# Gated linear attention and a mixture of experts on one core: scores ahead of the key transposes, ranks two steps late, first scans and checks by tile, and later weights

## The chip, the core and the metric

The kernel runs on one core of one Trainium2 chip. A core has five engines, each with an instruction queue of its own: TensorE (PE in the profile, with its weight loads as PEld), VectorE (DVE), ScalarE (ACT), GpSimd (POOL) and SyncE (SP), which here only issues transfers. Transfers are carried out by 16 DMA engines. The metric is the device time of one execution, in microseconds (us).

## What is computed

```python
def _attn_ref(q, k, v, alpha):            # each (4, 8, 768, 48): batch, head, time, width
    for t in range(S):
        state = alpha[:, :, t, :, None] * state + np.einsum('bhd,bhe->bhde', k[:, :, t], v[:, :, t])
        y[:, :, t] = np.einsum('bhd,bhde->bhe', q[:, :, t], state)

def _moe_ref(x, w_skip, w_gate, w1, w2):  # x: 3072 rows of 384
    do_compute = x @ w_skip > 0
    xc = x[do_compute]
    e_idx = np.argmax(xc @ w_gate, axis=1)                 # one of 8 experts
    gate_w = softmax(xc @ w_gate)[e_idx]
    for e in range(E):
        h = np.maximum(xc[mask] @ w1[e], 0.0)              # 384 -> 1024
        y[mask] = gate_w[mask, None] * (h @ w2[e])         # 1024 -> 384
    out[do_compute] = xc + y                               # the other rows stay x
```

The rows of attention, heads side by side, are the x of the experts.

## The kernel before

**Tiles.** Time is cut into 6 chunks of 128. A tile i is one chunk (i // 4) of one batch (i % 4) with all its 8 heads: 24 tiles. Two tiles make a pair j = i // 2, 12 pairs, and four tiles make a cycle, after which the next chunk of the same batch follows. Eight heads lie as four columns (p) of two partition halves (h): 48 rows from partition 0, 48 from partition 64, so that 112 partitions are spanned.

**A tile's arithmetic.** Scans over the decays give their running products from the left (`prefix`, tile pfx) and from the right (`suffix`, sfx), both on the DVE. GpSimd multiplies k by sfx (`scale_k`) and q by pfx (`scale_q`). Then PE computes k times q (`scores`, into ps_s), the DVE copies its causal part through a mask into the buffer st (`causal`), PE adds st times v (`intra`) and q times the state of the earlier chunks (`inter`) into ps_y. For the state, PE turns k (`turn_k`: transposes into ps_k, which ACT copies to kt), multiplies kt by v (`outer`, into ps_v), and the DVE adds the old state and multiplies by the chunk's total decay (`carry`). Of the output, ACT copies ps_y to xt, PE turns it to rows (`rows`, again into ps_k, of which there is one buffer), ACT copies it to x, and SP stores x.

**Routing.** Tiles are routed in groups (four at a time up to tile 16, then smaller). `logits` multiplies xt by the gate's weights wg, `route` takes nine short DVE instructions and one exponential on ACT (called one at a time by `tick`), `rank` counts with PE which place of its expert's list each row has, `slots` turns that into addresses, and `scatter` (GpSimd, an indirect DMA) writes row numbers into the lists xs in DRAM. `inspect` adds up on ACT how far the decays of a pair lie outside 0 to 1, two operations over 112x1024 into a scratch tile junk; the sums decide at the end whether a general path has to run (it doesn't here).

**Experts.** After the last tile `experts` loads the lists (`metas`), gathers the listed rows from the output (`gather`), turns them (`turn`), and computes `up` and `down` for each expert, 1 first. Weights come by `fetch` (raw pieces of 384 KB) and are split by `split` into a high part (ACT) and a low part (DVE or GpSimd). Each of the products with the experts' weights is three products of parts.

**Order.** The program is scheduled by hand: every engine carries out its instructions in the order in which the code issues them. `attention_begin` sets up and starts pair 0 and pair 1, then `step(i)` is called for the 24 tiles. In step i stand, in this order: on even i the loads of pair j + 3, the store of tile i - 2, one weight piece, turn_k, scores and causal of tile i + 1, on even i suffix and scale_k of pair j + 2, then inter(i), logits where a group is complete, outer(i), intra(i), rows(i - 1), on odd i prefix, scale_q, carry and inspect (of pair j + 3), the route, and at last rank and slots of a group that was complete one step before, and scatters. `constants_late` comes before inspect of the first three pairs, at the end of `attention_begin`. w1 and w2 of the first expert are fetched from step 3 on, w1 split on GpSimd from step 8 on, and the second w1 is fetched from step 22 on, behind the stores of those steps in SP's queue. The names in the order below end in numbers that mark a buffer (dec_138, _139 and _140 are the three decay buffers).

Of the kernel before, what the change touches and what calls it, by code (L numbers as in the profile page):

```python
# [10 lines left out]
F32 = mybir.dt.float32  # L11
# [12 lines left out]
P = 128  # L24
# [38 lines left out]
class Kernel:  # L63
# [12 lines left out]
    def constants_first(self):  # L76
# [9 lines left out]
        self.odd = const.tile([P, 2, NJ], F32, name="odd")  # L86
# [22 lines left out]
    def constants_late(self):  # L109
# [22 lines left out]
        self.wg = const.tile([P, NP, 32], F32, name="wg")  # L132
        nc.gpsimd.memset(self.wg, 0.0)
        for h in range(2):
            nc.sync.dma_start(out=self.wg[64 * h:64 * h + D, :, 0:E + 1], in_=self.w9[h])

# [14 lines left out]
    def constants_slots(self):  # L151
# [5 lines left out]
        nc.gpsimd.tensor_copy(self.slots1, slots_i)  # L157

# [55 lines left out]
    def scan_pools(self, st):  # L214
# [6 lines left out]
        self.junk = sfix.tile([P, NS, P], BF16, name="junk")  # L221
# [37 lines left out]
    def load_qk(self, j, t=None):  # L259
        nc, w = self.nc, self.pair(j)  # L260
        flat = w["qk"].rearrange("p t a s -> p t (a s)")
        for t in range(2) if t is None else (t,):
            if j < NFIRST:
                nc.sync.dma_start(out=flat[:PD, t], in_=self.qk0[j, :, t])
            else:
                for h in range(2):
                    nc.sync.dma_start(out=flat[64 * h:64 * h + D, t], in_=self.qk[j - NFIRST, h, :, t])
# [17 lines left out]
    def prefix(self, j, t0=0, t1=2):  # L285
# [7 lines left out]
        nc.vector.memset(dec[:, :, 0:1], 0.0)  # L293
# [15 lines left out]
    def inspect(self, j):  # L309

        dec = self.pair(j)["dec"][:PD, 0:2 * W1].rearrange("p (a s) -> p a s", s=SEG)[:, :, 2:]
        for n, (scale, bias) in enumerate(((1.0, -1.0), (-1.0, 0.0))):
            self.nc.scalar.activation(out=self.junk[:PD], in_=dec, func=AF.Relu, scale=scale, bias=bias,  # L313
                                      accum_out=self.odd[:PD, n, j:j + 1])
# [67 lines left out]
    def carry(self, j):  # L382
# [6 lines left out]
        if 2 * j >= B:  # L389
            nc.vector.tensor_tensor(pv, pv, state, ALU.add)  # L390
        nc.vector.tensor_tensor(state, pv, self.pair(j + 2)["total"][:PD].to_broadcast([PD, NS, D]), ALU.mult)
# [237 lines left out]
    def metas(self):  # L629

        self.meta = self.mp.tile([P, E, NB, 2], F32, name="meta")
        for e in (1, 0, *range(2, E)):
# [283 lines left out]
    def attention_begin(self):  # L916
        nc = self.nc
        for t in range(2):
            self.load_dec(0, t)
            self.load_qk(0, t)  # L920
        self.load_dec(1)
        self.load_v(0)
        self.load_qk(1)
        self.load_v(1)
        self.warm_up(WARM0)
        self.constants_scan()
        self.constants_pool()
        self.clear_buffers()
        self.load_dec(2)
        self.load_qk(2)  # L930
        self.load_v(2)
        for t in range(2):
            self.suffix(0, t, t + 1)
            self.scale_k(t)
            self.prefix(0, t, t + 1)
            self.scale_q(t, nc.vector)
            if t == 0:
# [220 lines left out]
```

## Time and profile before

| | |
|---|---|
| median of 3 runs | 332.57 us (331.17 to 335.27) |
| the profiled run | 332.18 us, its span 330.4 us |
| PE busy | 279.1 us (84%) |
| DVE busy | 211.4 us (64%) |
| ACT busy | 150.5 us (46%) |
| POOL busy | 127.0 us (38%) |
| transfers | 56.52 MB, mean 171 GB/s |

The span is what the profiler saw of one execution, from the first to the last instruction; the run's time holds a little more around it. Busy shares are averages over stages with different limits, so they say little by themselves. The views that follow later are: busy time by window, an engine's waits with what ended them, the chain of work that ended last, groups of equal instructions, the timeline of an engine, and the table of DMA issues. In them L323 is line 323 of the kernel before, `a<-b` is what an instruction writes and reads, and the clock is the share of TensorE's full speed that was granted.

### The profile page before, as it was taken

The page shows a single profiled execution, that of the slowest core. Times are in us where ns is not written, and L with a number is a line of the kernel's source. Part 1 is how long each engine was busy: PE and PEld are TensorE (multiplying, and loading weights), DVE is VectorE, ACT ScalarE, POOL GpSimd, SP SyncE. Part 2 cuts the span into 40 slices and gives each one's busy share as a digit, 9 for nine tenths or more (in the row PEclk, how much of TensorE's full clock was granted, in tenths as well). Part 3 has the DMA queues.
Part 4 walks back from the last instruction along what each step waited for, and adds up shares of the span by engine and source line. Part 5 has one row for each costly group of instructions (what it writes and reads, how often), then busy time and mean ns, then how long its engine had stood idle before and what let it go on. Part 6 is the DMA issues. An engine that isn't in the chain of part 4 may idle for free.

```text
span 330.4 us, 7415 instructions
## 1 busy us (share of the span) xinstructions
PE 279.1 (84%) x2937; PEld 254.8 (77%) x2937; DVE 211.4 (64%) x362; ACT 150.5 (46%) x333; POOL 127.0 (38%) x134
## 2 busy tenths in 40 slices
PE   8705895997797789598999579999999999999990
PEld 8604674776576667487799479999999999999990
DVE  5951796477677657668553665757585787758530
ACT  6155655255354254434430733736464637465510
POOL 3390355265656548557271165050403122110111
PEclk9955999599799699779999699999999999999996
DMA  7989989599887574011264097383939284755000
GB/s 192 264 203 243 216 227 290 154 226 257 211 199 202 170 151 125 27 41 35 67 152 101 2 284 273 113 301 115 307 103 320 112 279 180 222 205 192 35 26 19
DMA packets 28379, 56.52 MB, mean 171 GB/s; under 512 B 7192, under 2 KB 13792, under 8 KB 28336
## 3 DMA queue, kind: packets, MB, share of 16 engines
q1 hardware_dynamic: 25392, 50.89, 54.6%
q0 software_dynamic: 2944, 5.07, 4.4%
q8 instruction: 25, 0.41, 0.6%
q14 instruction: 18, 0.15, 0.2%
HBM read 49.09 MB, written 8.50 MB: 174 GB/s over the span
## 4 chain that ended last, share of the span: by engine, by line
PE 62%; DMA 11%; issue 8%; ACT 6%; DVE 5%; POOL 5%; SPq 0%; POOLq 0%; DVEq 0%
PE ps_o L691 19%; PE ps_h L676 18%; PE ps_s L323 6%; PE ps_y L362 5%; DMA xs<-idg,slot 4%; DMA dec<-in_dec_dram 3%; ACT junk L313 3%; PE ps_y L353 3%; PE ps_k L336 3%; PE ps_v L379 2%; DVE pfx L296 2%; DMA qk<-in_qk_dram 2%; PE ps_n L428 2%; POOL xs L518 1%; DMA xr<-out_dram,meta 1%
## 5 line engine op out<-in xcount | busy, mean ns | idle before, releaser
L329 DVE COPY_PREDICATED st<-mask,ps_s 128x1024 f32<-128x1024 uint8 x24 | 31.5, 1315 | 37.3 <-PE ps_s L323 37.2
L700 POOL DMA_INDIRECT out_dram<-o,meta x16 | 16.1, 1004 | 97.0 <-DVE o L698 96.4
L691 PE MATMUL ps_o<-w2h,hh 128*128 128x384 f32 x128 | 44.6, 349 | 3.2 <-ACT w2h L609 3.2
L691 PE MATMUL ps_o<-w2l,hh 128*128 128x384 f32 x128 | 44.3, 346 | 0.4 <-DVE w2l L611 0.3
L691 PE MATMUL ps_o<-w2h,hl 128*128 128x384 f32 x128 | 43.9, 343 | 0.0
L680 ACT ACTIVATE hh<-ps_h 128x512 fp32r<-128x512 f32 x32 | 19.2, 599 | 47.2 <-PE ps_h L676 47.2
L307 POOL TENSOR_TENSOR qk<-qk,sfx 112x512 f32<-112x512 f32 x24 | 28.0, 1183 | 32.4 <-issue 13.2
L303 POOL TENSOR_TENSOR qk<-qk,pfx 112x512 f32<-112x512 f32 x22 | 25.5, 1179 | 36.9 <-DVE pfx L296 36.9
L681 DVE SCALAR_TENSOR_TENSOR hl<-ps_h,hh 128x512 fp32r<-128x512 f32 x32 | 22.1, 692 | 27.4 <-ACT hh L680 27.3
L366 ACT COPY xt<-ps_y 112x256 f32<-112x256 f32 x48 | 15.5, 376 | 51.2 <-PE ps_y L362 51.2
L611 DVE TENSOR_TENSOR w2l<-raw,w2h 128x512 fp32r<-128x512 f32 x48 | 31.5, 683 | 8.3 <-ACT w2h L609 8.3
L676 PE MATMUL ps_h<-xh,w1h 128*128 128x256 f32 x192 | 33.6, 284 | 0.6 <-ACT xh L576 0.6
L676 PE MATMUL ps_h<-xh,w1l 128*128 128x256 f32 x192 | 33.4, 283 | 0.0
L676 PE MATMUL ps_h<-xl,w1h 128*128 128x256 f32 x192 | 33.4, 283 | 0.0
L323 PE MATMUL ps_s<-qk 48*128 48x128 f32 x384 | 31.7, 310 | 1.1 <-POOL qk L303 0.6
L609 ACT CAST w2h<-raw 128x512 fp32r<-128x512 f32 x48 | 28.0, 617 | 8.4 <-DMA out_dram<-x 8.4
L362 PE MATMUL ps_y<-st,v 128*64 128x128 f32 x384 | 31.8, 304 | 0.0
L279 DVE TENSOR_TENSOR_SCAN sfx<-dec,ps_t 112x1041 f32<-112x1041 f32 (+2 forms) x13 | 27.8, 2141 | 4.4 <-DMA dec<-in_dec_dram 2.8
L336 PE MATMUL ps_k<-ident,qk 112*128 112x112 f32 x80 | 12.4, 281 | 21.4 <-issue 16.0
L323 PEld LDWEIGHTS ps_s<-qk 48*128 48x128 f32 x384 | 26.6, 210 | 4.7 <-POOL qk L303 0.8
L541 POOL DMA_INDIRECT xr<-out_dram,meta x18 | 20.1, 1119 | 24.7 <-DVE hl L681 13.8
L296 DVE TENSOR_TENSOR_SCAN pfx<-dec,ps_t 112x1040 f32<-112x1040 f32 (+1 forms) x13 | 28.0, 2154 | 1.1
(156 smaller groups left out, 570.6 us busy)
## 6 DMA issues: line engine op xcount, KB each, us to landing
raw<-in_w_dram SPq DMA_DIRECT2D x64, 384.0 KB, 4.5
qk<-in_qk_dram SPq DMA_DIRECT2D x32, 192.0 KB, 6.5
v<-in_v_dram SPq DMA_DIRECT2D x12, 384.0 KB, 7.0
out_dram<-x SPq DMA_DIRECT2D x24, 192.0 KB, 4.1
qk<-in_qk_dram SPq DMA_DIRECT2D x8, 448.0 KB, 9.9
dec<-in_dec_dram SPq DMA_DIRECT2D x12, 232.8 KB, 4.9
dec<-in_dec_dram SPq DMA_DIRECT2D x12, 229.2 KB, 5.1
out_dram<-xr SPq DMA_DIRECT2D x3, 192.0 KB, 4.8
```

Of the source, the lines that this page charges most:

```text
L279: self.nc.vector.tensor_tensor_scan(w["sfx"][:PD, s][:, ::-1], w["dec"][:PD, s][:, ::-1], self.top[:PD].to_broadcast([PD, s.stop - s.start ...
L296: nc.vector.tensor_tensor_scan(w["pfx"][:PD, s], w["dec"][:PD, s], self.top[:PD].to_broadcast([PD, s.stop - s.start]), 1.0, ALU.mult, ALU.max)
L303: (eng or self.nc.gpsimd).tensor_tensor(w["qh"][:PD], w["qh"][:PD], w["pfx"][:PD], ALU.mult)
L307: (eng or self.nc.gpsimd).tensor_tensor(w["kh"][:PD], w["kh"][:PD], w["sfx"][:PD], ALU.mult)
L323: nc.tensor.matmul(ps[:, h, p * P:(p + 1) * P], lhsT=kh[r, p, :], rhs=qh[r, p, :], start=True, stop=True)
L329: self.nc.vector.copy_predicated(w["st"], self.mask, w["ps"])
L336: nc.tensor.transpose(ps[:, p, :], w["kh"][:PD, p, :], self.ident[:PD, :PD])
L362: nc.tensor.matmul(self.place(i, h, p), lhsT=w["v"][:, o:o + 64], rhs=w["st"][:, h, p * P:(p + 1) * P], start=(i < B and p < 2), stop=(p > ...
L609: nc.scalar.copy(out=hi[:, s], in_=raw[:, s])
L611: eng.tensor_tensor(lo[:, s], raw[:, s], hi[:, s].bitcast(F32), ALU.subtract)
L676: nc.tensor.matmul(ps[:, u, :], lhsT=a[:, k, f * P:(f + 1) * P], rhs=b[:, k, :], start=(n == 0), stop=(n == len(order) - 1))
L691: nc.tensor.matmul(ps, lhsT=a[:, f, js], rhs=b[:, f, :], start=(n == 0), stop=(n == 3 * FT - 1))
```

## The change

It moves much and computes the same. In the order of the program:

- q and k are laid out in DRAM so that a row of a transfer is 2 KB (q or k of one tile) where it was 4 KB (both). For pairs 0 and 1 each is a transfer of its own, k first; later pairs keep two transfers per tile, each now with two rows of 2 KB per partition. The gate's weights wg are padded on the host and come as one load, where GpSimd cleared the tile and two loads filled it.
- `constants_late` moves ahead of the scans, and in `attention_begin` pair 0 and pair 1 are scanned by tile; the second half of pair 1 is scanned in step 0 and the suffix of pair 2 in step 1. scale_q of tile 1 goes from the DVE to GpSimd.
- `prefix` writes its zero column with an ACT copy in place of a DVE memset.
- `inspect` takes one tile (112x512) in each step, where it took a pair in each second one.
- In each step scores come before turn_k.
- For the groups up to tile 16, rank and slots come two steps after the group is complete, between inter and outer, where they came one step after it, at the step's end. The DVE finishes the route (`tick(99)`) at each odd step.
- In `carry` the DVE adds, and GpSimd multiplies by the total.
- The first expert's weights are fetched from step 9 on, one piece a step, and w1 is split from step 19 on with the DVE, four calls a step. The second w1 is fetched in `experts`, behind the loads of the lists of experts 1 and 0 and ahead of those of the other six.

```diff
     def prefix(self, j, t0=0, t1=2):
...
-        nc.vector.memset(dec[:, :, 0:1], 0.0)
+        nc.scalar.copy(out=dec[:, :, 0:1], in_=nc.const_aps.tensor(0.0, [PD, (t1 - t0) * NP, 1], F32))
...
-    def inspect(self, j):
+    def inspect(self, i):
-        dec = self.pair(j)["dec"][:PD, 0:2 * W1].rearrange("p (a s) -> p a s", s=SEG)[:, :, 2:]
+        j, t = divmod(i, 2)
+        dec = self.pair(j)["dec"][:PD, t * W1:(t + 1) * W1].rearrange("p (a s) -> p a s", s=SEG)[:, :, 2:]
...
     def carry(self, j):
...
-        if 2 * j >= B:
-            nc.vector.tensor_tensor(pv, pv, state, ALU.add)
-        nc.vector.tensor_tensor(state, pv, self.pair(j + 2)["total"][:PD].to_broadcast([PD, NS, D]), ALU.mult)
+        total = self.pair(j + 2)["total"][:PD].to_broadcast([PD, NS, D])
+        if 2 * j < B:
+            nc.vector.tensor_tensor(state, pv, total, ALU.mult)
+            return
+        nc.vector.tensor_tensor(state, pv, state, ALU.add)
+        nc.gpsimd.tensor_tensor(state, state, total, ALU.mult)
...
     def step(self, i):
...
-        if i == 3:
+        if i == 9:
             self.fetches = chain(self.fetch(0, "w1"), self.fetch(0, "w2"))
...
-        if i == LATE + 4:
-            self.fetches = self.fetch(1, "w1")
-        for _ in range(2 if i >= LATE + 4 else 1):
-            next(self.fetches, None)
+        next(self.fetches, None)
...
-        if i == 8:
-            self.splits = self.split(0, "w1", nc.gpsimd)
+        if i == LATE + 1:
+            self.splits = self.split(0, "w1", nc.vector)
...
         if i + 1 < NT:
+            self.scores(i + 1)
             self.turn_k(i + 1)
-            self.scores(i + 1)
             self.causal(i + 1)
...
         self.inter(i)
...
+        done = ends.get(i - 2)
+        if done and done[1] < LATE:
+            self.tick(99)
+            self.rank(done)
+            self.small = self.slots(done)
         g = ends.get(i)
         if g:
             self.logits(g)
         self.outer(i)
...
             self.carry(j)
-            if j + 3 < NJ:
-                self.inspect(j + 3)
+        for n in (i + 2, i + 4) if i < 2 else (i + 4,):
+            if n < NT:
+                self.inspect(n)
...
         done = ends.get(i - 1)
-        if done:
+        if done and done[1] >= LATE:
...
-        self.tick(99 if i >= LATE else 3 if t else 1)
-        if i >= 8:
+        self.tick(99 if t or i >= LATE else 1)
+        for _ in range(4):
             next(self.splits, None)
...
     def experts(self):
-        self.metas()
+        self.metas((1, 0))
+        for _ in self.fetch(1, "w1"):
+            pass
+        self.metas(range(2, E))
```

On ACT, at the end of the first tiles' setting up, the order before is this (rtot is the reciprocal total that `prefix` keeps, L118 to L121 are late constants, L313 is inspect, L338 the copy of turned keys):

```order
L295 COPY rtot<-dec_139 112x8
L118 CAST tri<-tri_f 128x128
L119 CAST one_b<-ones_f 128x128
L120 ACTIVATE tri_n<-tri_f 128x128
L121 ACTIVATE one_n<-ones_f 128x128
L313 ACTIVATE junk,odd<-dec_138 112x1024 x2
L313 ACTIVATE junk,odd<-dec_139 112x1024 x2
L313 ACTIVATE junk,odd<-dec_140 112x1024 x2
L338 COPY kt<-ps_k 128x448
L366 COPY xt<-ps_y 112x256 x2
```

And this is it in the changed kernel (L295 writes a zero column, L297 rtot, L316 is inspect, L341 the copy of turned keys):

```order
L121 ACTIVATE one_n<-ones_f 128x128
L295 COPY dec_138<-const-float32-0.0 112x4
L297 COPY rtot<-dec_138 112x4
L341 COPY kt<-ps_k 128x448
L295 COPY dec_138<-const-float32-0.0 112x4
L297 COPY rtot<-dec_138 112x4
L316 ACTIVATE junk,odd<-dec_138 112x512 x2
L295 COPY dec_139<-const-float32-0.0 112x4
L297 COPY rtot<-dec_139 112x4
L316 ACTIVATE junk,odd<-dec_138 112x512 x2
L341 COPY kt<-ps_k 128x448
```

The constants now lie ahead of the first scan's zero column, looks of one tile lie between the scans, and the copy of turned keys no longer has six looks at whole pairs ahead of it.

On PE, where the first group is ranked, the order before has the rank at the end of step 5, ahead of the transposes and scores of tile 7 (tiles 6 and 7 are in qk_104):

```order
L493 MATMUL ps_n<-mg_287,one_b 128x8
L494 LDWEIGHTS tri
L494 MATMUL ps_n<-mg_287,tri 128x32
L336 MATMUL ps_k<-ident,qk_104 128x112 x4
L323 MATMUL ps_s<-qk_104 128x128 x8
L353 MATMUL ps_y<-qk_104,state_110 64x128 x8
```

In the changed kernel (L404 is rows, L326 scores, L339 turn_k, L356 inter, L494 on the rank):

```order
L404 MATMUL ps_k<-ident,xt 128x112 x4
L326 MATMUL ps_s<-qk_104 128x128 x8
L339 MATMUL ps_k<-ident,qk_104 128x112 x4
L356 MATMUL ps_y<-qk_104,state_110 64x128 x8
L494 LDWEIGHTS one_b
L494 MATMUL ps_n<-base_row,one_b 128x32
```

Scores stand between the rows of the tile before and the transposes, and the rank has moved behind scores, transposes and inter of step 6.

On SP, at the end of attention, the order before is this (L411 stores a tile, L535 loads the first expert's list early, L597 fetches a weight piece, L633 loads the lists):

```order
L535 DMA meta_1878<-xs 128x2x2
L411 DMA out_dram<-x 128x384
L597 DMA raw<-in_w_dram 128x768 x2
L411 DMA out_dram<-x 128x384
L597 DMA raw<-in_w_dram 128x768 x2
L411 DMA out_dram<-x 128x384 x2
L633 DMA meta<-xs 128x2x2 x8
L597 DMA raw<-in_w_dram 128x768 x40
```

In the changed kernel (L417 stores, L541 the early list, L603 fetches, L640 lists):

```order
L541 DMA meta_1905<-xs 128x2x2
L417 DMA out_dram<-x 128x384 x4
L640 DMA meta<-xs 128x2x2 x2
L603 DMA raw<-in_w_dram 128x768 x4
L640 DMA meta<-xs 128x2x2 x6
L603 DMA raw<-in_w_dram 128x768 x40
```

The four pieces of the second w1 have moved behind the last four stores and the first two lists.

More of the change, by code (lines that the diff above doesn't have):

```diff
@@ L157, in constants_slots, with load_gates @@
         nc.gpsimd.tensor_copy(self.slots1, slots_i)
+    def load_gates(self):
+        self.wg = self.const.tile([P, NP, 32], F32, name="wg")
+        self.nc.sync.dma_start(out=self.wg[:PD], in_=self.w9)
     def clear(self):
@@ L220, in scan_pools @@
         self.sfxp = pool("sfxp", 3)
-        self.junk = sfix.tile([P, NS, P], BF16, name="junk")
+        self.junk = sfix.tile([P, NP, P], BF16, name="junk")
     def clear_buffers(self):
@@ L627, in expert_pools, with metas @@
             self.nc.vector.memset(t, 0.0)
-    def metas(self):
-        self.meta = self.mp.tile([P, E, NB, 2], F32, name="meta")
-        for e in (1, 0, *range(2, E)):
+    def metas(self, experts):
+        if 1 in experts:
+            self.meta = self.mp.tile([P, E, NB, 2], F32, name="meta")
+        for e in experts:
             ins = self.nc.sync.dma_start(out=self.meta[:, e], in_=self.slot_rows(e))
@@ L931, in attention_begin @@
         self.load_v(2)
[L932 to L937, printed above, removed]
-                self.turn_k(0)
-                self.scores(0)
-                self.warm_up(WARMB)
-        self.causal(0)
-        self.suffix(1)
-        for t in (2, 3):
-            self.scale_k(t)
-        self.prefix(1)
-        for t in (2, 3):
-            self.scale_q(t)
-        self.constants_late()
-        for j in range(3):
-            self.inspect(j)
+        self.suffix(0, 0, 1)
+        self.scale_k(0)
+        self.prefix(0, 0, 1)
+        self.scale_q(0, nc.vector)
+        self.scores(0)
+        self.turn_k(0)
+        self.warm_up(WARMB)
+        self.suffix(0, 1, 2)
+        self.scale_k(1)
+        self.prefix(0, 1, 2)
+        self.scale_q(1)
+        self.causal(0)
+        self.inspect(0)
+        self.suffix(1, 0, 1)
+        self.scale_k(2)
+        self.prefix(1, 0, 1)
+        self.scale_q(2)
+        self.inspect(1)
         self.todo, self.fetches, self.splits = [], iter(()), iter(())
@@ L983, in step @@
         if i + 1 < NT:
+            self.scores(i + 1)
             self.turn_k(i + 1)
-            self.scores(i + 1)
             self.causal(i + 1)
-        if t == 0:
-            if j + 2 < NJ:
-                self.tick(2)
-                self.suffix(j + 2)
-                for n in range(2):
-                    self.scale_k(2 * j + 4 + n)
+        if i == 0:
+            self.suffix(1, 1, 2)
+            self.scale_k(3)
+            self.prefix(1, 1, 2)
+            self.scale_q(3)
+        if i == 1:
+            self.scan_right(2)
+        if t == 0:
+            self.tick(2)
+            if i > 0 and j + 2 < NJ:
+                self.scan_right(j + 2)
             self.tick(2)
@@ L1002, in step @@
         self.outer(i)
+        if done and done[1] < LATE:
+            self.tick(99)
+            self.todo += range(*done)
         if g and g[0] >= LATE:
@@ L1134, in layouts @@
     w9n = w9.reshape(KT, P, E + 1).transpose(1, 0, 2)
-    w9 = w9.reshape(NP, 2, D, E + 1).transpose(1, 2, 0, 3)
+    w9p = np.zeros((PD, NP, 32), w9.dtype)
+    for h in range(2):
+        w9p[64 * h:64 * h + D, :, 0:E + 1] = w9.reshape(NP, 2, D, E + 1)[:, h].transpose(1, 0, 2)
     nat = np.stack([alpha, k, q, v], axis=2).reshape(B, NP, 2, 4, S, D).transpose(0, 1, 3, 2, 5, 4)
```

47 lines of the change are left out of this document (27 added, 20 removed).

## The prediction

> **What bounds the kernel now.** I read the busy time by stage first, then TensorE's waits, then the chain of work and the queues at each wait. The first table cuts the span by stage; its columns are the window, its length, the busy time and count of PE, PEld, DVE, ACT and POOL, the granted clock, the DMA engines' share and GB/s.
>
> ```profile
> 0.00:51.90 51.90, 34.36 (x429) 29.69 (x433) 32.34 (x34) 26.25 (x62) 22.54 (x37) 0.84 0.90 230
> 51.90:130.20 78.30, 63.05 (x986) 51.56 (x989) 53.52 (x76) 36.05 (x89) 44.28 (x42) 0.89 0.77 199
> 130.20:172.60 42.40, 36.99 (x526) 30.89 (x522) 27.53 (x75) 16.61 (x46) 24.05 (x23) 0.92 0.23 58
> 172.60:199.40 26.80, 21.55 (x126) 20.16 (x127) 14.70 (x28) 9.35 (x18) 8.38 (x9) 0.87 0.48 132
> 199.40:330.40 131.00, 123.18 (x882) 122.50 (x880) 83.30 (x151) 62.26 (x118) 27.72 (x26) 0.98 0.52 176
> ```
>
> The edges are the masked copies (L329) of tiles 6 and 18, and the first instructions of up for the first and the second expert. So attention's start takes 51.9 us for six tiles, three cycles of four tiles take 78.3 (26.1 each), the last six tiles 42.4, the join of attention and experts 26.8, the experts' body 131.0. The body is full of PE work and the diff doesn't touch it. In the other stages no engine is full, so waits carry them.
>
> TensorE's waits (total, times, longest):
>
> ```profile
> PE ps_k L336 <- issue: 16.0, 5, 13.6
> PE ps_n L488 <- DVE sl L473: 13.3, 4, 3.3
> PE ps_o L691 <- ACT w2h L609: 3.2, 1, 3.2
> ```
>
> One of 13.6 us in the start; four of 3.3 at the rank of a group; one of 3.2 in the join. What the wait of 13.6 stands on is seen on ACT, where the copy of turned keys that frees `ps_k` stands behind six junk operations of inspect:
>
> ```profile
> 27.93 0.19 ACT L313 ACTIVATION_READ_ACCUMULATOR junk<-dec 112x1 f32 x1
> 28.02 0.51 ACT L338 COPY kt<-ps_k 128x448 f32<-128x448 f32 x1
> ```
>
> Clock and transfers in three windows, same columns as above:
>
> ```profile
> 28.60:34.60 6.00, 5.96 (x54) 5.16 (x55) 2.90 (x4) 1.19 (x4) 0.00 (x0) 0.50 1.02 251
> 58.50:65.30 6.80, 6.80 (x69) 5.56 (x68) 3.56 (x3) 1.18 (x3) 1.07 (x1) 0.50 0.55 163
> 192.90:194.90 2.00, 0.34 (x4) 0.10 (x2) 1.97 (x5) 0.48 (x1) 1.53 (x2) 1.00 1.01 373
> ```
>
> After the long wait, and after a rank's wait of 3.3, PE runs at clock 0.50 for six or seven us. After the gap of 1.9 us that ends at 194.9 it doesn't (1.00). The Trainium skill, "TensorE: Matmul & The Clock Gate", section "Why this matters for your kernels", asks for no idle gap above some 3 us; the trace agrees, with 3.3 on one side and 1.9 on the other.
>
> **The start.** The DVE has 32.34 us of work before tile 6's copy and can begin when the first decay is in:
>
> ```profile
> 3.79 1.24 DVE L279 TENSOR_TENSOR_SCAN sfx<-dec,ps_t 112x521 f32<-112x521 f32 x1 [2.76 <-DMA dec<-in_dec_dram]
> ```
>
> The change takes one multiply off it (`scale_q(1)`, of 512 columns like the split's subtraction in the row below, 0.68) and the memsets (an estimate of 0.4), so 31.2 us are left.
>
> ```profile
> L611 DVE TENSOR_TENSOR w2l<-raw,w2h 128x512 fp32r<-128x512 f32 x48 | 31.5, 683 | 8.3 <-ACT w2h L609 8.3
> ```
>
> Moved ahead of the scans, the late constants put four casts on ACT before the first zero column; inspect by tile halves what one look blocks ACT for. The new wait is that each prefix scan follows an ACT copy of the zero column, in ACT's order. My count over the six first prefixes of what the scan waits there: 2.1 behind clears and casts, 1.2 behind the first `kt`, then 0.4, 0.6 and 1.1 behind row copies and looks, 5.4 in all. 3.8 + 31.2 + 5.4 = 40.4 for tile 6, against 51.9: -11.5. That is if loads keep up. The window moved 230 x 51.9 = 11.9 MB. Three weight pieces of 0.39 MB leave it (w1(0) and w2(0) now begin in step 9), so 10.7 remain, and at the saturated 251 GB/s of 28.6 to 34.6 these take 42.6: -9.3. I take -9.5, since the q and k pieces at issue are the very loads of that window; bounds -4 (a wait of some 5 us for loads stays) and -11.5. The tile's transposes behind its scores, and `wg` as one load (SP no longer waits for GpSimd's memset), lie under the scans.
>
> **The three cycles.** A row of the chain is start, length and what ran:
>
> ```profile
> 74.11 0.54 PE ps_v L379 x13
> 74.64 0.95 PE ps_y L362 x16
> 75.59 0.53 PE ps_k L398 x4
> 76.12 0.11 PE ps_n L438
> 76.24 0.54 issue
> 76.77 0.57 PE ps_k L336 x4
> 77.35 1.09 PE ps_s L323 x16
> 78.44 0.60 PE ps_y L353 x16
> ```
>
> The 0.54 of issue is the copy of x out of the one `ps_k` buffer, ahead of the transposes. With scores first it is covered by scores (1.09): 0.5 less in each step whose chain runs there, two in four. At the rank the chain is:
>
> ```profile
> 56.23 1.15 ACT junk L313 x2
> 57.38 0.09 ACT ex L470
> 57.47 0.02 issue
> 57.49 0.19 DVE mg L472
> ```
>
> The exponential stands behind four instructions of inspect. Two steps late the ranks wait for less, and for the DVE rather than ACT. DVE's pieces in these cycles, and GpSimd's:
>
> ```profile
> L329 DVE COPY_PREDICATED st<-mask,ps_s 128x1024 f32<-128x1024 uint8 x13 | 17.1, 1316 | 23.4 <-PE ps_s L323 23.3
> L296 DVE TENSOR_TENSOR_SCAN pfx<-dec,ps_t 112x1040 f32<-112x1040 f32 x6 | 13.9, 2320 | 0.6
> L279 DVE TENSOR_TENSOR_SCAN sfx<-dec,ps_t 112x1041 f32<-112x1041 f32 x6 | 13.8, 2303 | 0.0
> L391 DVE TENSOR_TENSOR state<-ps_v,sfx 112x384 f32<-112x384 f32 x6 | 3.4, 559 | 0.2
> ```
> ```profile
> L307 POOL TENSOR_TENSOR qk<-qk,sfx 112x512 f32<-112x512 f32 x13 | 15.1, 1183 | 13.9 <-issue 9.9 <-DVE sfx L279 2.8 <-PE ps_n L438 1.2
> ```
>
> A new loop sets the period of a pair. At an odd step the scores end; then turn 0.57, inter 0.60, outer 0.54, intra 0.95, rows 0.53 on PE, the copy of x 0.5 (the 0.54 above) and the zero column 0.2 (as the accumulator's 0.19) on ACT, 3.9 with handover. Only then can the prefix scan start; before, it needed no PE result of the step. Then reciprocal 0.2 and scan 2.32, the carry's add 0.55, the next masked copy 1.32, which frees `ps_s`, and scores 1.09: 9.4 us a pair. One pair of a cycle carries nine short route instructions on the DVE (0.19 each, 1.5 of them in the loop), 10.9; the other carries logits on PE, half of their 1 us hidden, 9.9. A cycle is 20.8, and 3 x (26.1 - 20.8) = -15.9. In it the rank still waits some 2 us: PE is there 5.5 us after the odd scores' end (next scores at 4.3, then turn and inter 1.2), the route's result at 7.4. That is on the harmless side of the clock's edge. GpSimd's new multiply is estimated at 1183 x 384 / 512 = 0.89 a pair, ends long before the inter that reads the state, and with two scalings of k and q each (4 x 1.18) and scatters leaves GpSimd under 8.5 of 10 us. I take -15. Bounds -18 (no wait in the rank) and -8 (each prefix waits 0.8 more, and each rank's wait again halves the clock for 5 us: 6 x 0.8 + 3 x 2.5 = 12, less what overlaps).
>
> **Tiles 18 to 23 and the join.** Tiles 18 to 20 hold one pair of the cycle's kind, which 2.5 us leave by the same loop. w1(0)'s split moves from GpSimd in step 8 on to the DVE in steps 19 to 23: 6 or more of its subtractions are no longer covered by a waiting engine, x 0.68, less what lies in DVE's 35% of idle time: +1.5 (0.5 to 4). Together -1, bounds -2.5 and +2.
>
> In the join, the raws of w1(1) are issued before the last stores:
>
> ```profile
> 169.28 0.92 SPq L597 DMA_DIRECT2D raw<-in_w_dram  x2
> 170.30 0.86 SPq L411 DMA_DIRECT2D out_dram<-x  x2
> ```
> The chain then runs from the last scatter over the meta to the gather:
>
> ```profile
> 173.93 11.71 DMA xs<-idg,slot
> ...
> 186.10 1.78 DMA meta<-xs
> ...
> 190.07 4.74 DMA xr<-out_dram,meta
> ```
> The table of DMA issues has the median of all scatters (count, us to landing):
>
> ```profile
> xs<-idg,slot POOLq DMA_INDIRECT x24, 5.4
> ```
>
> The last scatter lands 11.71 us after its issue, in the company of those raws; the median of all is 5.4. With the raws behind the two first metas, 11.7 - 5.4 = -6.3. The floor of the join is PE's 21.55 less 3.4 for the half of seven us at clock 0.50, plus 2 for the gather: 20.1, so the next bound comes right there. The two gathers now run beside the raws, at some 1 us more: -5.5, bounds -2.5 (the scatter stays at 9) and -9.
>
> **Sum** against the profiled run (span 330.4, 332.18 with 1.8 around it, 0.4 under the median): -9.5 - 15 - 1 - 5.5 = -31, span 299.4, time 301 us. All good ends give -41, 291; all bad ends -4 - 8 + 2 - 2.5 = -12.5, 320; ends don't come together, so 293 to 317.
>
> **Rivals.**
> - *ACT's order is worse than counted.* The zero column stands behind kt, xt and x copies and looks, each 0.4 to 1.2 us. Another 2.4 us (two looks with accumulators) in each of eleven prefixes, not hidden, is +26: 327 at the worst, about 318 if two in three are hidden. For it: ACT is in order and the look of 112x512 remains in the step; against: ACT is idle half the stage (36.05 of 78.3).
> - *Pieces are no faster.* Two rows of 2 KB in place of one of 4 KB may saturate at the same 251 GB/s. A pair then brings 0.46 + 0.79 + 0.39 MB and a store of 0.39, with a weight piece of 0.39 per step up to 2.8 MB, 11.2 us for a pair with weights, where I have 10.4: +0.8 x 5 pairs and +5 at the start, about 309. The Trainium skill speaks against the change here: "DMA: Bandwidth & Descriptors", section "Rules for kernel authors", wants one large transfer in place of many. By that nothing would be gained from smaller pieces; the trace bears it out in part, as the 3 KB weight pieces ran at 373 GB/s where the mix with 4 KB rows had 251 at the same share.
> - *The landing stays.* If the last scatter takes 11 us for its small writes and not for the raws, the join gives 1 in place of 5.5: 305.5.
> - *The clock (slower than before).* More frequent waits of some 2 us may keep PE at 0.50, as one of 3.3 does now. PE's 55 us or so of attention work that now run at 1.00 would then take as long again, less its idle time of 10 us a cycle: from some 65 us at half clock on, the gain of 31 is gone; with all of attention so, 301 + 45 = 346. Against: the 1.9 us gap without any fall. The Trainium skill, the same clock page, section "A second HAM failure mode: psum-queue depth-cycling", tells of such a kernel; here no row shows it.
>
> **How the numbers follow.** The forecast has 0.5, ACT's order 0.2, the loads 0.12, the landing 0.1, the clock 0.05, and 0.03 is for others. 2% is about what a measurement of this kernel can tell from no change: 325.9 and 339.2. Only the worst of ACT's order and of the clock lie above 325.9: faster 0.88, same 0.07, slower 0.05. The range 293 to 317 takes in the forecast, loads, landing and the milder half of ACT's order.
>
> **What would show it.** PE's wait of 13.6 is gone and tile 6's copy starts at 41 to 43. Tile 6 to tile 18 takes 62 to 64 us; prefix scans begin 3.9 after the odd scores, released by ACT's copy of zeros. Ranks wait about 2 us, with clock 1.00 behind them. The last scatter lands within 6 us, and the casts of w2(1) don't wait. up for the second expert starts at 167 to 169. I am wrong if a prefix waits over 6 us for ACT, if the clock stays below 0.9 in the cycles, or if the body is longer than 132.

## The result, and the profile after

The changed kernel takes 314.71 us in the median of 4 runs (312.46 to 317.09); the kernel before took 333.92 (331.17 to 336.25) beside it. The ratio is 0.945, with a 95% interval of 0.933 to 0.957: faster, by some 19 us where 31 were forecast. Measured again in another session it took 312.29 (308.71 to 317.71), a ratio of 0.935 (0.926 to 0.944). One execution of a kernel differs from the next by up to 4% here, so times are medians, and a stage is read from one profiled execution with its clock beside it.

The same table by stage as before, for the changed kernel: window, length, busy time and count of PE, PEld, DVE, ACT and POOL, granted clock, share of the DMA engines, GB/s. The edges are the same events: masked copies of tiles 6 and 18, up's first instructions for the first and second expert.

```profile
0.00:42.05 42.05, 35.19 (x422) 30.56 (x423) 31.10 (x31) 26.67 (x83) 21.54 (x35) 0.88 1.01 237
42.05:104.35 62.30, 55.38 (x982) 45.56 (x983) 48.25 (x65) 36.12 (x115) 43.75 (x43) 1.00 1.02 265
104.35:158.48 54.13, 42.80 (x530) 35.10 (x529) 31.43 (x79) 22.01 (x64) 27.91 (x26) 0.81 0.17 55
158.48:179.28 20.80, 20.75 (x127) 20.31 (x128) 12.38 (x25) 9.54 (x18) 7.55 (x7) 0.85 0.62 184
179.28:310.70 131.42, 123.58 (x881) 122.67 (x880) 84.91 (x155) 62.06 (x118) 27.67 (x26) 0.99 0.52 177
```

Subtracting the lengths from those of before gives the account of the whole difference, 330.4 - 310.7 = 19.7 us:

| stage | before | after | difference | forecast |
|---|---|---|---|---|
| start, to tile 6 | 51.90 | 42.05 | -9.85 | -9.5 |
| three cycles | 78.30 | 62.30 | -16.0 | -15 |
| tiles 18 to 23, to up | 42.40 | 54.13 | +11.7 | -1 |
| join, up to up | 26.80 | 20.80 | -6.0 | -5.5 |
| experts' body | 131.00 | 131.42 | +0.4 | 0 |

Four stages came out within 1 us in this execution. One was missed by 12.7, and by subtraction that is the whole error; the experiments below share it out differently. TensorE's waits, in the same columns as before (total, times, longest):

```profile
PE ps_n L494 <- DVE sl L479: 7.9, 4, 2.0
PE ps_s L326 <- POOL state L397: 5.0, 1, 5.0
PE ps_k L404 <- ACT kt L341: 2.2, 1, 2.2
PE ps_h L683 <- DVE xl L583: 2.1, 1, 2.1
```

The wait of 13.6 us is gone and the ranks wait 2.0 us each, as forecast. New is a wait of 5.0 for the scores of tile 22. The clock around it, and at the start of up, in windows:

```profile
108.00:111.60 3.60, 1.65 (x30) 1.24 (x27) 3.23 (x7) 2.04 (x8) 1.43 (x2) 1.00 0.20 69
123.70:128.60 4.90, 0.02 (x2) 0.00 (x0) 4.87 (x8) 3.13 (x8) 4.39 (x4) 0.85 0.11 40
128.60:132.00 3.40, 3.33 (x34) 2.81 (x35) 3.29 (x5) 0.00 (x0) 2.79 (x3) 0.50 0.01 0
138.80:142.20 3.40, 3.40 (x36) 2.57 (x35) 2.33 (x3) 1.13 (x3) 1.05 (x2) 0.50 0.17 59
158.50:161.90 3.40, 3.40 (x16) 3.40 (x17) 2.59 (x7) 0.00 (x0) 0.97 (x1) 0.50 0.01 0
```

Behind the rank's wait (108.0 to 111.6) the clock is full. In the gap of 4.9 us the DVE is busy for 4.87 of it, and behind it PE runs at half clock, still so at 142 though it is busy all the time. What the DVE does there is in its timeline (start, length, line, operation, in brackets the idle time before it and what ended it):

```profile
117.34 1.30 DVE L332 COPY_PREDICATED st<-mask,ps_s 128x1024 f32<-128x1024 uint8 x1
118.54 0.19 DVE L296 RECIPROCAL dec<-sfx 112x8 f32<-112x8 f32 x1
121.64 2.32 DVE L298 TENSOR_TENSOR_SCAN pfx<-dec,ps_t 112x1040 f32<-112x1040 f32 x1 [2.92 <-ACT rtot L297]
...
124.62 2.75 DVE L617 TENSOR_TENSOR w1l<-raw,w1h 128x512 fp32r<-128x512 f32 x2
127.29 1.28 DVE L332 COPY_PREDICATED st<-mask,ps_s 128x1024 f32<-128x1024 uint8 x1
```

And on PE:

```profile
128.67 1.65 PE L326 MATMUL ps_s<-qk 48*128 48x128 f32 x12 [4.95 <-POOL state L397]
```

The scores of tile 22 need the one buffer ps_s, which the masked copy of tile 21 frees at 127.29 + 1.28 = 128.57; they start at 128.67. The wait bears GpSimd's name, whose multiply ended about then, but it is the DVE that they waited for. Ahead of that copy stand 2.92 us of waiting for ACT's zero column (the row names L297, the copy right behind it on ACT; with the zero column alone moved off ACT, below, this wait is gone), the prefix scan, and two subtractions of the split that the change moved to the DVE. These took 2.75 us, 1.38 each in place of 0.68: GpSimd multiplied in the same time. The Trainium skill, "GPSIMD Engine Reference", section "1. Specifications", says that GpSimd's ways to the on-chip memory are shared with the DVE, in contention where a DVE instruction reads two inputs there; this subtraction does, and the trace agrees.

So the first theory was that the split's place makes the gap, the gap halves the clock, and the half clock is the 12.7 us of the miss. The rivals: the clock falls there anyhow; the DVE's work costs what it costs wherever it stands; or the join was won for another reason than forecast.

### The profile page after: what moved, and what is told of

It is laid out like the page before. It is cut to its first block, busy times and chain, and to the rows that moved or that the text cites. A ratio compares the mean times of both kernels' runs of the same rounds, so it can differ in the third digit from the quotient of the medians.

```text
span 310.7 us, 7465 instructions
## 1 busy us (share of the span) xinstructions
PE 277.7 (89%) x2937; PEld 254.2 (82%) x2937; DVE 208.1 (67%) x349; ACT 156.4 (50%) x396; POOL 128.4 (41%) x136
## 4 chain that ended last, share of the span: by engine, by line
PE 51%; DVE 2%; issue 2%; ACT 1%; DMA 1%; POOL 0%; POOLq 0%; DVEq 0%
PE ps_h L683 22%; PE ps_o L698 19%; PE ps_v L564 2%; PE ps_y L365 2%; PE ps_s L326 1%; PE ps_x L668 1%; PE ps_n L434 1%; PE ps_y L356 1%; PE ps_k L404 1%; DMA raw<-in_w_dram 1%; DVE w1l L617 1%; DVE w2l L617 1%; DVE xl L583 1%; ACT hh L687 0%; PE ps_s L452 0%
## 5 line engine op out<-in xcount | busy, mean ns | idle before, releaser
L687 ACT ACTIVATE hh<-ps_h 128x512 fp32r<-128x512 f32 x32 | 19.1, 598 | 54.0 <-issue 26.5
L298 DVE TENSOR_TENSOR_SCAN pfx<-dec,ps_t 112x1040 f32<-112x1040 f32 (+1 forms) x14 | 28.2, 2011 | 24.2 <-ACT rtot L297 12.4
L698 PE MATMUL ps_o<-w2l,hh 128*128 128x384 f32 x128 | 42.9, 335 | 0.0
L305 POOL TENSOR_TENSOR qk<-qk,pfx 112x512 f32<-112x512 f32 x23 | 27.2, 1199 | 27.0 <-DVE pfx L298 27.0
L326 PE MATMUL ps_s<-qk 48*128 48x128 f32 x384 | 30.1, 300 | 6.6 <-POOL state L397 5.0
L683 PE MATMUL ps_h<-xh,w1l 128*128 128x256 f32 x192 | 34.7, 290 | 0.2 <-DVE w1l L617 0.2
L326 PEld LDWEIGHTS ps_s<-qk 48*128 48x128 f32 x384 | 25.3, 201 | 10.3 <-POOL state L397 5.2
L617 DVE TENSOR_TENSOR w1l<-raw,w1h 128x512 fp32r<-128x512 f32 x48 | 31.7, 714 | 0.0
L316 ACT ACTIVATE junk<-dec 112x512 bf16<-112x512 f32 x48 | 30.6, 638 | 0.8
L683 PEld LDWEIGHTS ps_h<-xh,w1h 128*128 128x128 f32 x192 | 29.1, 199 | 2.3 <-ACT xh L582 2.2
L524 POOL DMA_INDIRECT xs<-idg,slot x24 | 24.8, 1035 | 14.3 <-issue 9.4
L365 PE MATMUL ps_y<-st,v 128*64 128x128 f32 x384 | 30.1, 295 | 0.0
```

The source lines that it names most:

```text
L298: nc.vector.tensor_tensor_scan(w["pfx"][:PD, s], w["dec"][:PD, s], self.top[:PD].to_broadcast([PD, s.stop - s.start]), 1.0, ALU.mult, ALU.max)
L305: (eng or self.nc.gpsimd).tensor_tensor(w["qh"][:PD], w["qh"][:PD], w["pfx"][:PD], ALU.mult)
L326: nc.tensor.matmul(ps[:, h, p * P:(p + 1) * P], lhsT=kh[r, p, :], rhs=qh[r, p, :], start=True, stop=True)
L365: nc.tensor.matmul(self.place(i, h, p), lhsT=w["v"][:, o:o + 64], rhs=w["st"][:, h, p * P:(p + 1) * P], start=(i < B and p < 2), stop=(p > ...
L524: ins = nc.gpsimd.indirect_dma_start(out=self.xs[:, :], out_offset=bass.IndirectOffsetOnAxis(ap=self.slot[:, i, :], axis=0), in_=self.idg[ ...
L617: eng.tensor_tensor(lo[:, s], raw[:, s], hi[:, s].bitcast(F32), ALU.subtract)
```

## The experiments

The runs were made in three sessions, and the kernel before differs by less than 1 us among them, so times are compared across them. The last column is the execution from which the stages are read, which need not be the median one.

| run | us, median (lowest to highest) | profiled |
|---|---|---|
| before, in the three sessions | 331.55, 332.17, 332.44 | |
| changed, again | 312.29 (308.71 to 317.71) | 317.71 |
| split from step 21 | 307.98 (307.13 to 314.42) | 314.42 |
| zero column on the DVE | 297.65 (295.68 to 302.19) | 295.68 |
| gap filled with matmuls | 312.39 (310.01 to 315.07) | 312.19 |
| second w1 early | 311.88 (309.25 to 315.81) | 315.81 |
| zero column and split | 302.54 (297.60 to 304.44) | 301.80 |
| the same, three late scatters left out | 295.81 (292.97 to 303.07) | 292.97 |
| rows of 4 KB | 311.97 (309.95 to 322.27) | 322.27 |
| zero column, split spread out | 304.12 (301.95 to 304.67) | 303.78 |
| ranks one step late | 336.34 (333.82 to 338.55) | 336.36 |
| constants and looks back | 328.93 (320.96 to 330.40) | 330.40 |
| transposes first | 322.66 (319.23 to 326.86) | 319.23 |

**The split two steps later.**

```diff
-        if i == LATE + 1:
+        if i == LATE + 3:
             self.splits = self.split(0, "w1", nc.vector)
```

> The changed kernel with one move: the first w1's split begins in step 21 in place of 19, still on the DVE, four calls a step; everything ahead of it is as it was. Theory (the split's two subtractions, 2.75 us ahead of tile 21's masked copy, make PE's gap 4.95 us long, and so halve the clock for 20 us): the gap is 2.2 us, the clock stays at 1.00 behind it, tile 18 to up's first instruction takes 42 to 46 us in place of 54.1, time about 304 to 306. Rival 1 (the clock falls in the last tiles whatever the gap, since their steps hold little PE work): 51 or more for the stage, 312 to 315. Rival 2 (the split costs its 8 us of DVE and ACT time wherever it stands in the last tiles): 52 to 54, 313 to 315.

**The gap filled.** The same waits, but PE has something to do in the gap.

```diff
+        if i == LATE + 3:
+            self.warm_up(18)
         if i + 1 < NT:
             self.scores(i + 1)
```

> The changed kernel with 18 matmuls of zeros (the form of its own warm-up) in PE's gap ahead of tile 22's scores; their results are read by nobody. No wait is shortened, only the clock is kept. Theory (the loss of the last tiles is the half clock and not the wait): clock 1.00 behind the gap, the stage from tile 18 to up falls from 54.1 to 44 to 47 us, time 304 to 308. Rival (the last tiles are bound by DVE, ACT or GpSimd, the clock only follows): 52 to 54 us, 313 to 315.

Both did to their stage what the theory said. Of the kernel with the later split, the stage from tile 18 to up and the join:

```profile
111.50:153.44 41.94, 34.75 (x529) 29.01 (x529) 30.38 (x79) 22.11 (x64) 25.81 (x25) 1.00 0.20 61
153.44:181.16 27.72, 20.38 (x127) 19.52 (x127) 14.55 (x28) 9.74 (x18) 8.00 (x8) 0.88 0.49 149
```

Of the kernel with the gap filled, the same two stages:

```profile
106.15:151.78 45.63, 40.37 (x565) 34.26 (x565) 30.89 (x78) 22.10 (x64) 26.66 (x25) 0.96 0.17 51
151.78:179.56 27.78, 19.75 (x126) 19.10 (x127) 13.93 (x28) 9.63 (x18) 8.35 (x8) 0.88 0.49 147
```

The stage falls from 54.1 to 41.9 and 45.6. But filling the gap is worth nothing in time (312.39 against 312.29), and the later split 4.3. The join gives back what the stage wins: 27.8 and 27.7 in place of 20.8. The half clock was hiding another bound, and the join of the changed kernel was short because the stage ahead of it was long. The other profiles agree: wherever all scatters are done and the stage takes 42 to 47 us, the join takes 23 to 29; where it takes 53 to 62, the join takes 19 to 21. From tile 18 to the second expert's up it is 69.2 us before (42.4 + 26.8), 74.9 changed (73.3 in its second profile), 69.7 with the later split and 73.4 with the gap filled. Net of the join, then, the half clock cost at most 1.5 us, which is no more than the changed kernel's own two profiles differ by, and the split's place 3.7 to 5.3, not 12.

**The raws of the second w1.** The forecast's reason for the join was that these loads held up the last scatter. Here they stand ahead of the last stores again, as before the change.

```diff
+        if i == LATE + 4:
+            self.fetches = self.fetch(1, "w1")
+        for _ in range(2 if i >= LATE + 4 else 1):
+            next(self.fetches, None)
-        next(self.fetches, None)
...
         self.metas((1, 0))
-        for _ in self.fetch(1, "w1"):
-            pass
```

> The changed kernel with the second w1 fetched from step 22 on again, two pieces a step, ahead of the last stores. Theory (the raws are what kept the last scatter and the stores from landing): from the first expert's up to the second's takes 25 to 27 us in place of 20.8, PE waits 3 us or more there, time 319 to 321. Rival (the landing was slow for other reasons, or the gain came from elsewhere): 20 to 22 us, 314 to 316.

The time did not move: 311.88 in the median, where the theory had 319 to 321. The stages of the profiled execution, from tile 18 to up and the join, did:

```profile
107.60:154.10 46.50, 38.53 (x529) 32.05 (x528) 31.10 (x79) 22.12 (x64) 27.58 (x26) 0.89 0.28 73
154.10:183.19 29.09, 21.72 (x127) 19.90 (x127) 14.62 (x28) 9.34 (x18) 8.55 (x8) 0.82 0.51 136
```

The join of 29.1 in place of 20.8 is even more than the theory's 25 to 27. But in this execution half clock lasted 6.5 us behind the gap and not 20, so the stage ahead is short, as it is with the gap filled; and there the join takes 27.8 with no raw on its way. So the long join goes with the short stage, and the raws account for 1.3 us of it at most. The last scatter says the same: with the raws ahead it takes 9.68 us to land; with the gap filled, where the DMA engines' share is 0.03 meanwhile, it takes 10.14, nearly the 11.71 of before. The chain of the kernel with the gap filled (start, length, what ran):

```profile
153.15 10.14 DMA xs<-idg,slot
...
163.47 2.13 DMA meta<-xs
...
166.44 6.39 DMA xr<-out_dram,meta
```

GpSimd's timeline of the same kernel suggests why, in the issues of the late tiles' scatters:

```profile
146.69 1.03 POOL L524 DMA_INDIRECT xs<-idg,slot  x1 [0.30 <-DVE slot L520]
148.02 1.00 POOL L524 DMA_INDIRECT xs<-idg,slot  x1 [0.30 <-issue]
...
153.15 0.97 POOL L524 DMA_INDIRECT xs<-idg,slot  x1 [0.30 <-issue]
```

Six of them (the two ends and one are shown) leave 1.3 us apart. From the first issue to the last landing pass 163.3 - 146.7 = 16.6 us, 2.8 for each of six on the mean. In the changed kernel half clock on PE spread them out, so that GpSimd had been idle for 3 us when the last one left, and it landed in 4: it was issued at 159.28, and the list that waits for it was fetched at 163.22.

```profile
159.28 0.97 POOL L524 DMA_INDIRECT xs<-idg,slot  x1 [3.01 <-DVE idg L483]
```
```profile
163.22 0.89 SPq L640 DMA_DIRECT2D meta<-xs  x2
```

**The zero column on the DVE.**

```diff
-        nc.scalar.copy(out=dec[:, :, 0:1], in_=nc.const_aps.tensor(0.0, [PD, (t1 - t0) * NP, 1], F32))
+        nc.vector.memset(dec[:, :, 0:1], 0.0)
```

> The changed kernel with the zero column written by a DVE memset again, as before the change. Theory of the loop through ACT (in the cycles a prefix scan waits for an ACT copy that stands behind the copy of x, 24 us of such waits in all): each prefix starts up to 2.4 us earlier, a cycle falls from 20.8 towards PE's and DVE's work, 18.5 to 20; tile 21's masked copy no longer waits the 2.9 us, so PE's gap there falls below 3.3 and the clock holds; time 296 to 302. Rival (the waits are only slack: PE or the transfers, at a share of 1.02, set the cycle): the cycles stay at 20.5 or more and only the gap gains, 303 to 307; if the gap too is bound by something else, 313 to 315.

297.65 us, the lowest of all kernels that do the whole work: a ratio of 0.8985 to before (0.8855 to 0.9115). Its stages up to tile 18:

```profile
0.00:39.05 39.05, 34.08 (x422) 29.56 (x423) 31.51 (x37) 25.87 (x77) 22.57 (x36) 0.91 0.99 247
39.05:95.40 56.35, 55.38 (x982) 45.63 (x983) 49.01 (x69) 35.17 (x109) 44.12 (x44) 1.00 1.06 268
```

A cycle is 18.8 in place of 20.8 and PE is busy in 55.4 of 56.4 us: the loop through ACT was what set the cycle, and with it gone PE does. The rank's wait falls to 0.2. This part of the change cost some 15 us of what the rest had won. One sign of the expectation failed: the gap ahead of tile 22's scores is still 3.2 us, with the DVE busy throughout, and though it is below 3.3 the clock falls behind it, for 6.5 us (the wait, and two of these 6.5 us):

```profile
PE ps_s L326 <- POOL state L397: 3.2, 1, 3.2
```
```profile
121.00:123.00 2.00, 2.00 (x20) 1.67 (x18) 0.02 (x1) 0.53 (x2) 0.00 (x0) 0.50 0.05 4
```

**Both together, and with half of the late scatters.**

> The zero column on the DVE and the split from step 21 on together. Theory (the last six scatters pass their queue at some 2.4 us each, whatever PE does, so from the first of them to the second expert's up it takes 33 us; ahead of that the two gains add): no gap over 3.3 us, clock 1.00 until the join, the first late scatter leaves 2 to 4 us earlier than with the zero column alone, time 292 to 296. Rival (with the DVE free, PE bounds the last tiles and the join alike): 288 to 291. Rival (the gains overlap in full): 297 to 299.

```diff
     def scatter(self, i):
         nc = self.nc
+        if i >= NT - 3:
+            return
```

> As the run with both, but the scatters of tiles 21, 22 and 23 are left out: their rows reach no expert's list and keep attention's value. The experts' work is of fixed size and stays. Theory (each late scatter takes 2.4 us of its queue): the last of the remaining ones lands some 7 us earlier against the start of the first expert's up, the second expert's up follows after 20 to 22 us, PE's wait for the gather goes, time 5 to 7 us below the run with both. Rival (the last scatter is slow for a reason of its own, the loads or stores beside it or a fixed time to landing): it still lands 7 to 10 us after its issue, time at most 3 us below, by the earlier issue.

Both together were not better than the zero column alone (302.54, above all three ranges of the expectation): PE waited 3.8 us for ACT's copy of the logits, which itself stood idle for 2.0 us on something that the profile doesn't name, and half clock came back for 14 us. Why that copy was late stays open. The join tells what the second run was for. With all scatters, then with three:

```profile
144.83:168.31 23.48, 19.74 (x127) 19.18 (x127) 13.88 (x27) 9.73 (x18) 7.04 (x7) 0.93 0.60 173
```
```profile
142.19:159.94 17.75, 17.75 (x126) 17.70 (x127) 14.60 (x28) 9.45 (x18) 6.64 (x7) 1.00 0.73 220
```

With three scatters fewer PE works through the join without a pause, the join is 5.7 us shorter behind a stage of the same length (46.9 for 47.2), and the median is 6.7 us lower, though the ranges overlap. So the scatters set the join there. Not all of the theory stands, though: the last of the three still took 7 us from its issue to the list's fetch (135.46 to 142.70), so it isn't a matter of their number alone.

**The split spread out**, with the zero column on the DVE.

```diff
-        if i == LATE + 1:
+        if i == 11:
             self.splits = self.split(0, "w1", nc.vector)
...
-        for _ in range(4):
+        for _ in range(2 if i >= LATE else 1):
             next(self.splits, None)
```

> The zero column on the DVE, and the first w1's split on the DVE spread out: one call a step from step 11 on, two from step 18 on. Theory (a lump of splits on ACT or DVE in the last tiles makes PE's gap, spread out they lie in idle time; then the six late scatters set the join): no PE gap over 3.3 us after the start, cycles within 0.5 us of the run with the zero column alone (18.8), from tile 18's masked copy to the second expert's up 65 to 67 us in place of 67.7, time 292 to 296. Rival (cycles at 18.8 are full, the split's 8 us come on top of them): cycles of 19.5 or more, 297 to 301.

A miss: 304.12 lies above both ranges. Cycles are 19.3, at the edge of what the theory allows, and no gap ahead is over 1.8 us; yet the clock falls. Windows of that kernel: the stretch with the 1.8 us gap, the fall, and what follows:

```profile
113.00:117.00 4.00, 2.22 (x35) 1.87 (x33) 3.97 (x7) 2.73 (x8) 3.83 (x4) 1.00 0.13 49
117.00:120.00 3.00, 3.00 (x48) 2.24 (x45) 2.27 (x3) 0.39 (x1) 2.39 (x3) 0.67 0.06 6
...
123.00:147.00 24.00, 23.44 (x175) 19.94 (x176) 7.89 (x37) 5.42 (x16) 7.32 (x7) 0.50 0.14 44
```

With the later split a wait of 1.8 us in the same place (tile 22's scores) left the clock at 1.00. So a single gap's length doesn't decide it in these tiles, and the theory's bound of 3.3 falls. Between the last two windows, at half clock already, PE waits 2.6 us for ACT's copy of the logits; whether that wait is why the half clock lasts so long here wasn't tried.

**Parts of the change undone.** Ranks one step late at the step's end, the rest as changed:

```diff
-        done = ends.get(i - 2)
-        if done and done[1] < LATE:
-            self.tick(99)
-            self.rank(done)
-            self.small = self.slots(done)
...
         done = ends.get(i - 1)
-        if done and done[1] >= LATE:
+        if done:
             self.tick(99)
```

> The changed kernel with the ranks of the first five groups one step late at the step's end again, as before the change. Theory (the rank then stands in PE's order ahead of the next scores and waits for the DVE's prefix, add and route): waits of 3.5 to 4.5 us in place of 2.0, each followed by half clock, a cycle 2 to 3.5 us longer, time 319 to 324. Rival (looks of one tile and the route finished at odd steps already did it, the step more is worth nothing): cycles within 0.7 us, 312 to 315.

336.34 us, a ratio to before of 1.012 (1.008 to 1.016): without this part the change loses all it won. The ranks' waits, and the three cycles:

```profile
PE ps_n L494 <- DVE sl L479: 16.8, 4, 4.2
```
```profile
41.20:120.70 79.50, 65.54 (x983) 53.65 (x984) 49.12 (x66) 36.81 (x115) 43.66 (x43) 0.83 0.83 205
```

Waits of 4.2 in place of 2.0, clock 0.83 in place of 1.00, 26.5 us a cycle in place of 20.8. The direction was expected, the size was not: 336 us where 319 to 324 stood. A cycle is 5.7 us longer than in the first profile of the changed kernel and 3.5 longer than in its second, where 2 to 3.5 stood; and from tile 18 to the second up it takes 81.8 us in place of 74.9, of which the expectation had nothing.

Constants and looks behind the scans again:

```diff
-        self.constants_late()
         self.load_dec(2)
...
-        self.inspect(0)
...
         self.scale_q(2)
-        self.inspect(1)
+        self.constants_late()
+        for n in range(6):
+            self.inspect(n)
...
-        for n in (i + 2, i + 4) if i < 2 else (i + 4,):
+        for n in (i + 4,) if i >= 2 else ():
```

> The changed kernel with the late constants behind the scans of the first tiles again, and the looks of six tiles together behind them, on ACT ahead of the first copies that free PE's buffers. Theory (these made PE's 13.6 us gap): a gap of 6 us or more comes back, tile 6's masked copy is 5 to 9 us later than 42.1, time 317 to 323. Rival (the loads, at a share of 1.01, set the start): at most 2 us later, 312 to 316.

```profile
0.00:49.30 49.30, 35.25 (x423) 30.68 (x424) 30.89 (x32) 27.14 (x83) 21.41 (x35) 0.86 0.87 226
```

Tile 6 starts 7.2 us later, behind a PE wait of 9.6 for kt: the start's gain came from ACT's order. The median is 16.6 above the changed kernel, more than the start explains; but one execution of the four took 320.96, within the 317 to 323 that was expected, and the others 327.6 to 330.4. What lies beyond the start wasn't taken apart, so the price of this part is 7 us in the start, and open beyond it.

Rows of 4 KB (the layout, and whole tiles in one load, as before the change):

> The changed kernel with q and k in rows of 4 KB again, one load per tile for pairs 0 and 1 and two for the others, as before the change. Theory (small pieces make the loads faster, 251 GB/s at full share before): tile 6 begins its masked copy 2 to 4 us later than in the changed kernel and the time is 317 to 321. Rival (the DMA engines move the same 240 to 265 GB/s either way, and the loads' start only sets who goes first): within 1 us in the start, 313 to 316.

Tile 6 at 41.8 in place of 42.1, 311.97 us in place of 312.29: the smaller pieces are worth nothing.

Transposes first:

```diff
-            self.scores(i + 1)
             self.turn_k(i + 1)
+            self.scores(i + 1)
             self.causal(i + 1)
```

> The changed kernel with the key transposes ahead of the scores again in each step. Theory as predicted (scores cover the wait for the copy of x): two waits of 0.5 us come back a cycle, cycles 21.3 to 22, time 315 to 318. Rival (the loop through ACT: the transposes then lie outside of the path from the odd scores' end to the prefix): 0.57 less a pair, cycles 19.6 to 20.4, 308 to 312.

```profile
PE ps_k L339 <- ACT x L413: 5.3, 8, 0.9
```
```profile
42.30:111.20 68.90, 57.37 (x985) 46.79 (x989) 48.83 (x63) 36.39 (x114) 43.97 (x44) 0.98 0.99 250
```

The waits for the copy of x come back, eight of them for 5.3 us, and a cycle is 23.0. 322.66 us: scores ahead are worth 10, where I had reckoned 0.5 for each of two steps a cycle, 3 in all. The clock of 0.98 says that falls of the clock aren't the reason; what is stays open.

**The changed kernel again.**

> The changed kernel as it is, on the same chip as the three runs beside it. All theories: 312 to 316.

312.29, and its profiled execution fell to half clock behind each of the three ranks' waits in the cycles. The window up to the rank, and the next:

```profile
47.00:50.00 3.00, 1.03 (x29) 0.84 (x24) 2.80 (x9) 0.99 (x4) 1.61 (x2) 0.81 1.05 243
50.00:53.00 3.00, 3.00 (x38) 2.57 (x34) 3.00 (x3) 0.48 (x2) 1.51 (x2) 0.62 0.19 67
```

Its cycles took 69.1 us, those of the first profile 62.3. The waits are 2.0 to 2.4 us there, 2.0 in the first. The kernel with the gap filled has the same program in its cycles; its profiled execution, 312.19 us and so near the median, took 65.9 for them, with one fall behind a rank's wait.

## Why the prediction was right, and where it was wrong

- **Start, -9.5 for -9.85: the wait was right, the number luck in part.** Put back, the constants and looks bring a 9.6 us wait and 7.2 us, so the gain came from ACT's order, as forecast. But -9.5 was taken from the loads (10.7 MB at the saturated rate, 42.6 us). The window moved 237 GB/s x 42.05 us = 10.0 MB, and with the zero column on the DVE tile 6 comes at 39.05 at a share of 0.99: the loads weren't the limit, and that 42.6 met 42.05 is luck. Rows of 4 KB did as well, so the pieces were no part of the gain.
- **Cycles, -15 for -16.0: right in the sum of one execution.** Over the three executions above it is -16.0, -12.4 and -9.2. Of the parts undone one at a time, the ranks' step is the largest, 24 us with what follows it, then constants and looks with 17 by the medians, 7 of them in the start, and scores ahead with 10; together that is more than the change won, so they don't add, and the forecast's split among them isn't borne out. The loop from the odd scores over x and ACT's zero column to the prefix was there: taken out, a cycle falls from 20.8 to 18.8. What I called the harmless side of the clock's edge is the edge itself: waits of 2.0 to 2.4 us halved the clock behind none of the ranks in one execution, behind one and behind three in others.
- **Tiles 18 to 23, -1 for +11.7: the step that failed here.** It priced the moved split as "6 or more of its subtractions ... x 0.68, less what lies in DVE's 35% of idle time: +1.5 (0.5 to 4)". The work isn't the price: two subtractions at 1.38, behind a prefix that waits for ACT, stand ahead of the masked copy that frees the one ps_s, and make PE's gap of 4.95 us; half clock for 20 us follows (6.5 in the execution with the raws early). I had priced each DVE instruction by itself and not asked which buffer the next one frees. But not all of the 12.7 is the split's. With the later split this stage takes 41.9, as forecast, and stage and join together 69.7, where the forecast had 62.7 and the changed kernel 74.9 (73.3). So the split's place costs 3.7 to 5.3 us, and some 7 are the join's miss, which in the changed kernel shows under tiles 18 to 23.
- **Join, -5.5 for -6.0: the right number for a wrong reason.** That "the raws of w1(1) are issued before the last stores" was hardly a cause: put back, they leave the time as it is and the join 1.3 us longer than with no raw on its way (29.1 and 27.8). The last scatter lands 10 us after its issue either way when six leave together, and with three of them left out the join shrinks by 5.7; why the third then still takes 7 us isn't known. The join was short in the changed kernel because the stage ahead had been stretched at half clock. Had the tiles 18 to 23 gone as forecast, the join would have taken 27.7, and the whole gain would have been 31 less some 7, about 24, as an estimate; the later split measured 331.55 - 307.98 = 23.6.
- **The rivals.** ACT's order was worth 15 us when taken away. In the profiled executions 3.0 of it lie in the start and 5.9 in the cycles, where the forecast's sums held such waits, and 7.2 from tile 18 to the second up, where it held too little. The rival of the landing ("11 us for its small writes and not for the raws") was nearer to the truth than its chance of 0.1. As to the clock's rival, it came in some executions' cycles and not to the extent of its price.
- **Slips in the working.** The gap called 1.9 us is 1.7 in the list of TensorE's waits. For ACT's order, 318 is the sum with one prefix in three hidden; with two in three it is 301 + 26 / 3, about 310. The 10 us of idle time a cycle in the clock's rival aren't in the rows: (78.30 - 63.05) / 3 leaves 5.1. And pieces of 3 KB that ran faster than a mix with rows of 4 KB do not bear out a rule for large transfers.

## What to carry to other kernels

Where a queue is in order, ask of each moved instruction which buffer the instruction behind it frees and who waits for that; its own duration says little. Add up two neighbouring stages before calling one of them won: a stretch that is slowed may hide the bound of the next, and repairing it then pays only the difference. And a wait that is near the clock's edge is a cost in some executions, so it is worth taking away rather than putting just below.

## What the runs showed of the hardware

- Half clock outlasts its cause by very different times: 6.5 us behind a gap of 3.2 with the zero column on the DVE and behind one of 4.5 with the raws early, 14 with both edits, 20 in the changed kernel, 30 with the split spread out, where PE was busy in 23.44 of 24.0 us. The Trainium skill, "TensorE: Matmul & The Clock Gate", section "What's actually happening", has full speed back after about 3.4 us of sustained work; the measurement differs, and decides. What sets the length stays open, as does why waits of 1.8 and 2.0 us halve the clock in some executions and not in others.
- Of six indirect scatters of 128 rows, issued 1.3 us apart, the last lands 10 us after its own issue and 16.6 after the first one's; one that left 4.3 us after the scatter ahead of it took 4.
- Rows of 2 KB and of 4 KB loaded alike: 237 to 258 GB/s and 247 in the start, at a share of 0.99 to 1.01.
